# A decayed linear attention with two feed-forward layers: the work around each attention cell in another order of blocks

## The chip, the cores and the metric

The kernel runs on 1 core of one Trainium2 chip. The metric is device time in microseconds of that core; lower is better. Before the change it is 1261.89 us, the median of 3 runs (1261.34 to 1262.25).

## The reference

Three stages follow each other, all in float32, over 4 batches of 768 tokens (3072 tokens, 384 channels, which are 8 heads of 48).

```python
# attention: a state per batch and head, decayed by w, with a bonus u for the present token
cur = np.einsum('bhd,bhe->bhde', u[None] * kt, vt)
y[:, :, t] = np.einsum('bhd,bhde->bhe', rt, state + cur)
state = w[None, :, :, None] * state + np.einsum('bhd,bhe->bhde', kt, vt)
# first layer: 4 experts of 1024 hidden units, all used, weighted by normalised probabilities
h = np.maximum(x @ w1[e], 0.0)
out += p[:, e:e + 1] * (h @ w2[e])
# second layer: 2048 hidden units
h = x @ w_in
g = h * np.cos(h)
out = g @ w_out
```

## The kernel before, in words

The two layers are one stream of *items*. An item is a block of 128 hidden units for up to 512 tokens: three up matmul groups (`m_up`), a relu or a cosine, and, two or three items later, the down matmuls (`m_down`) into three accumulators. The loop over `n` issues the items in order. A product of float32 precision is made of three rounded ones: each operand is split into a high part, rounded by ScalarE, and a low part, the rest, taken by VectorE (`split`, L117 and L118, for x; L504 and L505 for weights, L608 and L609 for the hidden block, `gh` and `gl`). VectorE does the weights' low part in even items, GpSimd in odd ones, up to item 28. The first 8 items take weights and x as they are (`raw_w`, `x_raw`) and need no split. Items with `n` below about 30 have 256 tokens, later ones 512.

The attention is cut into 24 *cells* of 128 tokens of one batch; `i` counts a batch's cells, `b` the batches. The first two cells are worked before the loop (functions `b_...`). Their results are transposed on TensorE by `b_x` (L274), copied by ScalarE (L275), and are the x of the first items. Later cells are worked inside the loop: at item `ONE_AT[c]` TensorE gets the scores and the state of cell `c` and the outputs of cell `c - 1` (`a_one`, `a_visit`; L191, L177, L357, L368), between the item's own matmuls. A visit borrows the tile `hp` that the item does not use, so it waits for the `gl` of the item before. The other steps of a cell are put down in the table `steps`, by item, relative to `p`, the item of the cell before: `a_load_tok` and `a_load_t` load it, `a_kt` (GpSimd, L149) and `a_r` (VectorE, L145) apply the decay, `a_ru` (GpSimd, L153) the bonus, `a_rk` (VectorE, L157) takes the product of both, `a_kp` (VectorE, L166) the keys for the state, `a_sum` (VectorE, L161) the sum of the bonus. `wide` is true for cells 3 to 8, whose visits are 4 items apart; later visits are 3 apart. Within an item, `mix` places these steps between the matmuls; each engine works its own queue in the order in which it was written.

A visit's result goes to DRAM (`yd`). When the four batches of an `i` are done, `x_in` loads it back and queues the three splits of x, with a delay in items (a lag and a step for each of the three parts).

The splits in the loop's head are written before an item's matmuls, the splits of weights after 8 items at its end:

```python
if n < BLK - 3:
    raw_load(n + 3, nc.scalar)
if 2 <= n < BLK:
    w_loads(n - 1)
    w_splits(n - 3, nc.gpsimd if n % 2 else None)
```

Loads of the first blocks are issued from ScalarE's queue (up to three weight blocks and cells 3 to 5), the others from SP's. The tile pools `ps_d` and `ps_u` use the same banks one after the other; `ups2` are the two tiles `hp`.

Of the kernel before, what the change touches and what calls it, by code (L numbers as in the profile page):

```python
# [11 lines left out]
ACTF = mybir.ActivationFunctionType  # L12
ALU = mybir.AluOpType
# [13 lines left out]
def attention_moe_cos_mlp_kernel(  # L27
# [17 lines left out]
    nc = tc.nc  # L45
# [7 lines left out]
    C = 64  # L53
# [5 lines left out]
    BLK = 8  # L59
# [40 lines left out]
    pw = at_p.tile([128, HP, 129], F32, name="pw")  # L100
    w128 = at_p.tile([128, HP, 1], F32, name="w128")
# [12 lines left out]
    dense_ps = [ps_d.tile([128, 2, 512], F32, tag=t, name=f"{t}_ps") for t in ("ds", "dy")]  # L114
# [36 lines left out]
    def a_ru(c):  # L151
        t = ld[c]["tok"][:, 0:2]
        nc.gpsimd.tensor_tensor(out=t, in0=t, in1=uu_ch, op=ALU.mult)  # L153
# [81 lines left out]
    def b_mask(c):  # L235
        s_ = t_p.tile([128, 2, HP, C], F32, tag="s", name="s")
        by = ld[c]["ps"].rearrange("q c (p a t) -> q a c p t", p=HP, a=2)
        wide = [128, 2, HP, C]
        nc.vector.tensor_tensor(out=s_, in0=by[:, 0], in1=mask.unsqueeze(1).unsqueeze(1).to_broadcast(wide), op=ALU.mult)
        nc.vector.copy_predicated(  # L240
            out=s_, mask=eye.bitcast(I32).unsqueeze(1).unsqueeze(1).to_broadcast(wide), data=by[:, 1],
        )
        ld[c]["s"] = s_
# [28 lines left out]
    def b_x(c, px):  # L272
        for kk in range(KD):
            nc.tensor.transpose(px[:, kk * 128:kk * 128 + 128], ld[c]["yo"][:, kk * 128:kk * 128 + 128], ident)  # L274
        nc.scalar.activation(  # L275
            out=x_raw[:, :, c * 128:c * 128 + 128], in_=px[:, 0:DM].rearrange("q (k t) -> q k t", k=KD), func=ACTF.Copy
        )
# [17 lines left out]
    ups2 = []  # L295
# [117 lines left out]
    def x_in(i, j, lag, cols=slice(0, TB), step=None):  # L413
        src = acc[j].rearrange("q b d -> q (b d)").rearrange("q (k t) -> q k t", k=KD)
        nc.sync.dma_start(out=src[:, :, cols], in_=yd[i].rearrange("(k q) t -> q k t", k=KD)[:, :, cols])
        x_split(src, j, lag, cols, step or X_STEP)

    def x_split(src, j, lag, cols=slice(0, TB), step=None):
        for kk in range(KD):
            later.append((  # L420
                lag + (step or X_STEP)[kk],
                lambda kk=kk: split(xh[j][:, kk, cols], xl[j][:, kk, cols], src[:, kk, cols]),
            ))

    def a_x(c):
        b, i = cells[c]
        if b == B - 1 and i == 0:
            x_in(0, 0, X0_LAG, slice(256, 512), (0, 0, 0))
        if b == B - 1 and i == 1:
            x_in(1, 1, XT_LAG)  # L430
        ld.pop(c)

    NC_ = len(cells)
# [8 lines left out]
    on_pe = (a_one,)  # L442
    ONE_AT = {c: 4 * c - 6 for c in range(N_FIRST, 9)}
    ONE_AT.update({c: 29 + 3 * (c - 9) for c in range(9, NC_ + 1)})
    BEGIN = {3: ((a_load_tok, 0), (a_load_t, 0), (a_ru, 1)), 4: ((a_load_tok, 3), (a_load_t, 4), (a_ru, 5)), 5: ((a_load_tok, 6), (a_load_t, 7), (a_ru, 8))}

    def steps_of(c):
        at, p = ONE_AT[c], ONE_AT[c - 1]
        wide = at - p > 3
        two = ONE_AT.get(c - 2, 0)  # L450
        yield from BEGIN.get(c, ((a_load_tok, two - 1), (a_load_t, two), (a_ru, p - (2 if wide else 1))))
        yield from ((a_kt, p), (a_r, p + wide), (a_rk, p + 2), (a_kp, p + 2), (a_sum, p + 2 + wide))

    steps = {}
    for c in range(N_FIRST, NC_ + 1):
# [40 lines left out]
    def raw_load(q, eng=None):  # L496
        (eng or nc.sync).dma_start(out=raw_w[0, 0, q], in_=moe_wb[q])
# [22 lines left out]
    def w_loads(n):  # L520
        while w_nl[0] < min(n, len(w_keys)):
            w_load(w_keys[w_nl[0]])
            w_nl[0] += 1
# [196 lines left out]
    wu_a = const.tile([128, 128], mybir.dt.bfloat16, name="wu_a")  # L720
    wu_b = const.tile([128, 512], mybir.dt.bfloat16, name="wu_b")
# [133 lines left out]
    N_DEC = N_ATT + 4  # L855
    X_STEP = (0, 0, 1)
    X_LAG = 1
    XT_LAG = 2
    TAIL = 2
    Y_LAG = 1  # L860
    WARM_FIRST = 17
    X0_LAG = 2
# [21 lines left out]
    with tc.manual_schedule():  # L884
# [12 lines left out]
        raw_load(1)  # L897
        prob_load()
        raw_load(2)
        for c in range(N_FIRST):  # L900
            b_r(c)
            a_kt(c, nc.vector)
        nc.vector.tensor_tensor(out=w128, in0=pw[:, :, 2 * C:2 * C + 1], in1=pw[:, :, 2 * C:2 * C + 1], op=ALU.mult)
        for c in range(N_FIRST):
            b_ru(c)
        off = x_bank()
# [4 lines left out]
        b_score(1, dense_ps[0], off[:, HP * C:2 * HP * C])  # L911
        b_off(1)
        b_mask(1)
        a_ru(2)
        a_kt(2)
        b_in(0, dense_ps[1][:, :, 0:HD])
# [4 lines left out]
        b_in(1, pair_ps[:, :, 0:HD])  # L921
        b_y(1)
        b_x(0, dense_ps[0][:, 0])
        b_x(1, dense_ps[0][:, 1])
        a_r(2)
        a_rk(2)
        a_sum(2)
# [2 lines left out]
        ps_d_ctx.close()  # L930
        ps_u = ctx.enter_context(tc.tile_pool(name="ps_u", bufs=1, space=bass.MemoryType.PSUM))
        ups2 += [ps_u.tile([128, TB], F32, name=f"hp{x}") for x in range(2)]
        for hp in ups2:
            nc.tensor.matmul(hp[:, 256:512], wu_a, wu_b[:, 0:256], start=True, stop=True)
        ps_a = ctx.enter_context(tc.tile_pool(name="ps_a", bufs=1, space=bass.MemoryType.PSUM))
        downs = []
        pend = []
# [1 line left out]
        for n in range(NI + 4):  # L939
            live = n < NI  # L940
            moe2 = False
            if n < BLK - 3:
                raw_load(n + 3, nc.scalar)
            if 2 <= n < BLK:
                w_loads(n - 1)
                w_splits(n - 3, nc.gpsimd if n % 2 else None)
            if n == 3:
                prob_norm()
# [19 lines left out]
            if live:  # L968
# [21 lines left out]
                hp, ups = m_up(n)  # L990
# [247 lines left out]
```

## Time and profile before

| what | value |
|---|---|
| median of 3 runs | 1261.89 us |
| the profiled execution | 1262.03 us |
| its span, first to last instruction | 1260.3 us |
| TensorE (PE) busy | 1246.5 us, 99% of the span |
| VectorE (DVE) busy | 773.0 us, 61% |
| ScalarE (ACT) busy | 492.9 us, 39% |
| GpSimd (POOL) busy | 193.6 us, 15% |
| granted TensorE clock | 0.999 |

The profile is one execution. A line of its timeline gives the start, the length, the engine, the source line and the operation, what it writes and reads, and, in brackets, how long the engine was idle before it and what ended that. SPq and ACTq are the instructions by which these engines issue transfers. The whole attention lies in the first quarter of the span, up to about 310 us, and VectorE is busy for 219 of the first 300 us.

### The profile page before, as it was taken

How to read it: one execution, taken by the hardware profiler on the slowest of the kernel's cores; microseconds unless marked ns; L12 is line 12 of the kernel's file. 1: busy time of each engine (PE TensorE's matmuls, PEld its weight loads, DVE VectorE, ACT ScalarE, POOL GpSimd, SP SyncE). 2: the span in 40 equal slices, each digit the busy share in tenths (PEclk: the TensorE clock that was granted, in tenths of full speed). 3: DMA queues.
4: the chain of work that ended last, by engine and by line, in shares of the span. 5: the costliest groups of instructions: out<-in, count | busy, mean ns of one | idle time of the engine just before them, and what ended most of it. 6: DMA issues, size and time to landing. Idle time of an engine off the chain costs nothing.

```text
span 1260.3 us, 20498 instructions
## 1 busy us (share of the span) xinstructions
PE 1246.5 (99%) x8453; PEld 1038.8 (82%) x8453; DVE 773.0 (61%) x1259; ACT 492.9 (39%) x879; POOL 193.6 (15%) x190
## 2 busy tenths in 40 slices
PE   9999999999999999999999999999999999999997
PEld 7898888788888888888888888888888888888886
DVE  6897747766264464546645543326776777777665
ACT  4442313223221131112111222216777677767774
POOL 3664323421100000111111111112000100010100
PEclk9999999999999999999999999999999999999999
DMA  8635634444242243223331410123001400160601
GB/s 322 220 117 177 196 125 154 124 137 111 84 139 59 84 134 109 67 76 127 107 92 52 133 43 9 59 78 122 1 1 42 160 26 25 36 203 13 196 11 47
DMA packets 72501, 126.53 MB, mean 100 GB/s; under 512 B 23153, under 2 KB 44754, under 8 KB 72402
## 3 DMA queue, kind: packets, MB, share of 16 engines
q1 hardware_dynamic: 65634, 93.38, 23.6%
q0 software_dynamic: 4608, 25.17, 6.4%
q10 hardware_dynamic: 2160, 6.62, 1.5%
q8 instruction: 67, 1.10, 0.4%
q14 instruction: 32, 0.26, 0.1%
HBM read 101.90 MB, written 23.25 MB: 99 GB/s over the span
## 4 chain that ended last, share of the span: by engine, by line


## 5 line engine op out<-in xcount | busy, mean ns | idle before, releaser
L595 PE MATMUL hp<-xh,w 128*128 128x512 f32 (+1 forms) x888 | 341.3, 384 | 1.6 <-DVE gl L609 1.6
L596 PE MATMUL hp<-xl,w 128*128 128x512 f32 (+1 forms) x888 | 338.1, 381 | 0.5 <-DVE xl L118 0.5
L597 PE MATMUL hp<-xh,w 128*128 128x512 f32 (+1 forms) x888 | 337.9, 380 | 0.2 <-issue 0.2
L670 PE MATMUL a<-gh,w 128*128 128x512 f32 (+1 forms) x880 | 335.0, 381 | 0.0
L671 PE MATMUL a<-gh,w 128*128 128x512 f32 (+1 forms) x880 | 334.8, 380 | 0.0
L672 PE MATMUL a<-gl,w 128*128 128x512 f32 (+1 forms) x880 | 334.7, 380 | 0.0
L608 ACT ACTIVATE gh<-hp 128x512 fp32r<-128x512 f32 (+1 forms) x200 | 114.5, 573 | 539.7 <-PE hp L597 532.6
L609 DVE SCALAR_TENSOR_TENSOR gl<-hp,gh 128x512 fp32r<-128x512 f32 (+1 forms) x200 | 131.1, 657 | 299.5 <-ACT gh L608 298.8
L595 PEld LDWEIGHTS hp<-xh,w 128*128 128x128 f32 x888 | 166.9, 188 | 35.7 <-DVE gl L609 2.9
L597 PEld LDWEIGHTS hp<-xh,w 128*128 128x128 f32 x888 | 166.9, 188 | 32.1
L596 PEld LDWEIGHTS hp<-xl,w 128*128 128x128 f32 x888 | 167.0, 188 | 31.9 <-DVE xl L118 0.7
L670 PEld LDWEIGHTS a<-gh,w 128*128 128x128 f32 x880 | 165.5, 188 | 32.0 <-ACT rr L626 0.4
L672 PEld LDWEIGHTS a<-gl,w 128*128 128x128 f32 x880 | 165.5, 188 | 31.7
L671 PEld LDWEIGHTS a<-gh,w 128*128 128x128 f32 x880 | 165.5, 188 | 31.5
L693 POOL TENSOR_TENSOR acc<-acc,pm 128x512 f32<-128x512 f32 (+1 forms) x57 | 72.5, 1302 | 537.9 <-DVE pm L692 537.9
L628 DVE SCALAR_TENSOR_TENSOR hs<-rr,hs 128x512 f32<-128x512 f32 x96 | 67.4, 702 | 62.8 <-ACT rr L627 62.8
L626 ACT ACTIVATE rr<-rr 128x512 f32<-128x512 f32 x96 | 60.8, 633 | 86.4 <-DVE rr L621 86.4
L620 DVE SCALAR_TENSOR_TENSOR rr<-ni,hs 128x512 f32<-128x512 int32 x96 | 66.3, 691 | 45.6 <-ACT ni L619 45.6
L621 DVE SCALAR_TENSOR_TENSOR rr<-ni,rr 128x512 f32<-128x512 int32 x96 | 66.5, 692 | 3.3
L507 POOL DMA_DIRECT2D w<-dec_all x32 | 17.1, 535 | 333.0 <-PE a L672 332.1
L118 DVE TENSOR_TENSOR gl<-hs,gh 128x512 fp32r<-128x512 f32 x96 | 66.0, 688 | 0.7 <-ACT gh L117 0.7
L618 ACT ACTIVATE hs<-hp 128x512 f32<-128x512 f32 x96 | 57.2, 596 | 17.8 <-PE hp L597 17.6
(151 smaller groups left out, 1066.2 us busy)
## 6 DMA issues: line engine op xcount, KB each, us to landing
w<-dec_all POOLq DMA_DIRECT2D x32, 768.0 KB, 4.6
s<-in_moe_wb_dram SPq DMA_DIRECT2D x53, 384.0 KB, 4.0
draw<-in_moe_wb_dram SPq DMA_DIRECT2D x32, 384.0 KB, 4.3
dec_all<-dout SPq DMA_DIRECT2D x32, 384.0 KB, 3.0
tok<-in_tok_ch_dram SPq DMA_DIRECT2D x19, 576.0 KB, 5.4
rkt<-in_rkt_dram SPq DMA_DIRECT2D x21, 512.0 KB, 3.8
pb<-pn SPq DMA_DIRECT2D x24, 256.0 KB, 5.0
out_dram<-acc SPq DMA_DIRECT2D x17, 256.0 KB, 2.5
```

The lines of the kernel that those rows point to most:

```text
L595: nc.tensor.matmul(hp, wh[:, kk, :], x_h[:, kk, :], start=kk == 0, stop=False)
L596: nc.tensor.matmul(hp, wh[:, kk, :], x_l[:, kk, :], start=False, stop=False)
L597: nc.tensor.matmul(hp, wl[:, kk, :], x_h[:, kk, :], start=False, stop=kk == KD - 1)
L608: nc.scalar.activation(out=gh, in_=hp, func=ACTF.Relu)
L609: nc.vector.scalar_tensor_tensor(out=gl, in0=hp, scalar=0.0, in1=gh.bitcast(F32), op0=ALU.max, op1=ALU.subtract)
L620: nc.vector.scalar_tensor_tensor(out=rr, in0=ni, scalar=-PI2_HI, in1=hs, op0=ALU.mult, op1=ALU.add)
L621: nc.vector.scalar_tensor_tensor(out=rr, in0=ni, scalar=-PI2_LO, in1=rr, op0=ALU.mult, op1=ALU.add)
L628: nc.vector.scalar_tensor_tensor(out=hs, in0=rr, scalar=1.0, in1=hs, op0=ALU.subtract, op1=ALU.mult)
L670: nc.tensor.matmul(a, wh[:, ds], gh, start=q == 0, stop=False)
L671: nc.tensor.matmul(a, wl[:, ds], gh, start=False, stop=False)
L672: nc.tensor.matmul(a, wh[:, ds], gl, start=False, stop=q == BLK - 1)
L693: nc.gpsimd.tensor_tensor(out=o, in0=o, in1=m, op=ALU.add)
```

## The change

Eight edits; line numbers are those of the kernel before.

1. `b_x(1, ...)`: the transposes of the second cell go to the other tile, `dense_ps[1]`.
2. The two matmuls that fill columns 256 to 512 of the tiles `hp` (L934) are gone; two ScalarE copies in items 0 and 1 do it.
3. `w128` is computed after the masks of the first two cells.
4. Weight block 3 is loaded by SP ahead of the loop; blocks 4 to 7 by ScalarE's queue at items 2 to 5, one item later than before, and the weight loads that are split begin one item later.
5. Cell 3: loads at item 1 and bonus at item 2, each one item later.
6. `a_rk` for cells from 9 on one item earlier; unchanged for cells 3 to 8.
7. `a_kp` for cells 3 to 8 one item later; unchanged after that.
8. x parts: the third part of the second half of the first x one item later; the parts of the second x at lags 1, 2, 3, where they were at 2, 2, 3.

```diff
--- before.py
+++ after.py
@@ -425,9 +425,9 @@
     def a_x(c):
         b, i = cells[c]
         if b == B - 1 and i == 0:
-            x_in(0, 0, X0_LAG, slice(256, 512), (0, 0, 0))
+            x_in(0, 0, X0_LAG, slice(256, 512), (0, 0, 1))
         if b == B - 1 and i == 1:
-            x_in(1, 1, XT_LAG)
+            x_in(1, 1, XT_LAG, step=(0, 1, 2))
         ld.pop(c)
 
     NC_ = len(cells)
@@ -442,14 +442,14 @@
     on_pe = (a_one,)
     ONE_AT = {c: 4 * c - 6 for c in range(N_FIRST, 9)}
     ONE_AT.update({c: 29 + 3 * (c - 9) for c in range(9, NC_ + 1)})
-    BEGIN = {3: ((a_load_tok, 0), (a_load_t, 0), (a_ru, 1)), 4: ((a_load_tok, 3), (a_load_t, 4), (a_ru, 5)), 5: ((a_load_tok, 6), (a_load_t, 7), (a_ru, 8))}
+    BEGIN = {3: ((a_load_tok, 1), (a_load_t, 1), (a_ru, 2)), 4: ((a_load_tok, 3), (a_load_t, 4), (a_ru, 5)), 5: ((a_load_tok, 6), (a_load_t, 7), (a_ru, 8))}
 
     def steps_of(c):
         at, p = ONE_AT[c], ONE_AT[c - 1]
         wide = at - p > 3
         two = ONE_AT.get(c - 2, 0)
         yield from BEGIN.get(c, ((a_load_tok, two - 1), (a_load_t, two), (a_ru, p - (2 if wide else 1))))
-        yield from ((a_kt, p), (a_r, p + wide), (a_rk, p + 2), (a_kp, p + 2), (a_sum, p + 2 + wide))
+        yield from ((a_kt, p), (a_r, p + wide), (a_rk, p + 1 + wide), (a_kp, p + 2 + wide), (a_sum, p + 2 + wide))
 
     steps = {}
     for c in range(N_FIRST, NC_ + 1):
@@ -855,7 +855,7 @@
     N_DEC = N_ATT + 4
     X_STEP = (0, 0, 1)
     X_LAG = 1
-    XT_LAG = 2
+    XT_LAG = 1
     TAIL = 2
     Y_LAG = 1
     WARM_FIRST = 17
@@ -897,10 +897,10 @@
         raw_load(1)
         prob_load()
         raw_load(2)
+        raw_load(3)
         for c in range(N_FIRST):
             b_r(c)
             a_kt(c, nc.vector)
-        nc.vector.tensor_tensor(out=w128, in0=pw[:, :, 2 * C:2 * C + 1], in1=pw[:, :, 2 * C:2 * C + 1], op=ALU.mult)
         for c in range(N_FIRST):
             b_ru(c)
         off = x_bank()
@@ -911,6 +911,7 @@
         b_score(1, dense_ps[0], off[:, HP * C:2 * HP * C])
         b_off(1)
         b_mask(1)
+        nc.vector.tensor_tensor(out=w128, in0=pw[:, :, 2 * C:2 * C + 1], in1=pw[:, :, 2 * C:2 * C + 1], op=ALU.mult)
         a_ru(2)
         a_kt(2)
         b_in(0, dense_ps[1][:, :, 0:HD])
@@ -921,7 +922,7 @@
         b_in(1, pair_ps[:, :, 0:HD])
         b_y(1)
         b_x(0, dense_ps[0][:, 0])
-        b_x(1, dense_ps[0][:, 1])
+        b_x(1, dense_ps[1][:, 0])
         a_r(2)
         a_rk(2)
         a_sum(2)
@@ -930,8 +931,6 @@
         ps_d_ctx.close()
         ps_u = ctx.enter_context(tc.tile_pool(name="ps_u", bufs=1, space=bass.MemoryType.PSUM))
         ups2 += [ps_u.tile([128, TB], F32, name=f"hp{x}") for x in range(2)]
-        for hp in ups2:
-            nc.tensor.matmul(hp[:, 256:512], wu_a, wu_b[:, 0:256], start=True, stop=True)
         ps_a = ctx.enter_context(tc.tile_pool(name="ps_a", bufs=1, space=bass.MemoryType.PSUM))
         downs = []
         pend = []
@@ -939,10 +938,12 @@
         for n in range(NI + 4):
             live = n < NI
             moe2 = False
-            if n < BLK - 3:
-                raw_load(n + 3, nc.scalar)
-            if 2 <= n < BLK:
-                w_loads(n - 1)
+            if n < 2:
+                nc.scalar.activation(out=ups2[1 - n][:, 256:512], in_=wu_b[:, 0:256], func=ACTF.Copy)
+            if 2 <= n < BLK - 2:
+                raw_load(n + 2, nc.scalar)
+            if 3 <= n < BLK:
+                w_loads(n - 2)
                 w_splits(n - 3, nc.gpsimd if n % 2 else None)
             if n == 3:
                 prob_norm()
```

The order in which the instructions now stand shows it at three places.

VectorE's queue around items 4 to 6, where cell 3 is prepared (`kp` are the keys, `xl` the low parts of x, L505 a weight's low part). Before:

```order
L505 TENSOR_TENSOR w<-s,w 128x768
L118 TENSOR_TENSOR xl_99<-acc_106,xh_98 128x256
L157 TENSOR_TENSOR tok<-tok 128x384
L166 TENSOR_TENSOR kp_125<-tok,wk_ch 128x384
L118 TENSOR_TENSOR xl_99<-acc_106,xh_98 128x256
L161 TENSOR_REDUCE dsum<-tok 128x8
```

Now:

```order
L505 TENSOR_TENSOR w<-s,w 128x768
L118 TENSOR_TENSOR xl_99<-acc_106,xh_98 128x256
L157 TENSOR_TENSOR tok<-tok 128x384
L118 TENSOR_TENSOR xl_99<-acc_106,xh_98 128x256
L166 TENSOR_TENSOR kp_125<-tok,wk_ch 128x384
L161 TENSOR_REDUCE dsum<-tok 128x8
```

The keys of cell 3 have moved behind the second part of x.

ScalarE's queue at items 3 and 4 (L604 is the relu of a first item, L497 loads a block that stays as it is, L493 a block that L504 will split, L137 and L128 load a cell). Before:

```order
L497 DMA raw_xl_103<-in_moe_wb_dram 128x768
L493 DMA s<-in_moe_wb_dram 128x768
L137 DMA tok<-in_tok_ch_dram 128x1152
L604 ACTIVATE gh<-hp_355 128x256
L497 DMA raw_xl_103<-in_moe_wb_dram 128x768
L493 DMA s<-in_moe_wb_dram 128x768
L504 ACTIVATE w<-s 128x768
```

Now:

```order
L497 DMA raw_xh_102<-in_moe_wb_dram 128x768
L493 DMA s<-in_moe_wb_dram 128x768
L137 DMA tok<-in_tok_ch_dram 128x1152
L604 ACTIVATE gh<-hp_356 128x256
L497 DMA raw_xl_103<-in_moe_wb_dram 128x768
L493 DMA s<-in_moe_wb_dram 128x768
L504 ACTIVATE w<-s 128x768
```

The rows read alike, but each stands for the block before: in the upper list the first L493 loads weight block 1 and the second block 2, in the lower one block 0 and block 1. L504 here rounds block 0 in both.

VectorE's queue at items 23 to 25, where cell 8 is prepared. Before:

```order
L609 SCALAR_TENSOR_TENSOR gl<-hp_355,gh 128x256
L157 TENSOR_TENSOR tok<-tok 128x384
L166 TENSOR_TENSOR kp_127<-tok,wk_ch 128x384
L609 SCALAR_TENSOR_TENSOR gl<-hp_354,gh 128x256
L505 TENSOR_TENSOR w<-raw_xh_102,w 128x768
L161 TENSOR_REDUCE dsum<-tok 128x8
```

Now:

```order
L609 SCALAR_TENSOR_TENSOR gl<-hp_356,gh 128x256
L157 TENSOR_TENSOR tok<-tok 128x384
L609 SCALAR_TENSOR_TENSOR gl<-hp_355,gh 128x256
L505 TENSOR_TENSOR w<-raw_xh_102,w 128x768
L166 TENSOR_TENSOR kp_127<-tok,wk_ch 128x384
L161 TENSOR_REDUCE dsum<-tok 128x8
```

The keys of cell 8 have moved behind the low part of the hidden block and behind that of a weight; the same holds for cells 4 to 7, with or without the weight.

## Rows read from the trace of the kernel before

**Rows 1.** Page, part 1: busy time and share of the engines.
```profile
PE 1246.5 (99%) x8453; PEld 1038.8 (82%) x8453; DVE 773.0 (61%) x1259; ACT 492.9 (39%) x879; POOL 193.6 (15%) x190
```

**Rows 2.** Waits, TensorE: us in total, times, longest.
```profile
PE hp L595 <- DVE gl L609: 1.6, 3, 1.1
...
PE hp L357 <- DVE gl L609: 1.1, 2, 0.7
```

**Rows 3.** Timeline 13 to 16 us, ScalarE and TensorE: start, us, engine, operation, idle before.
```profile
13.28 0.49 ACT L275 ACTIVATE acc<-ds_ps 128x384 f32<-128x384 f32 x1
...
13.83 0.55 PE L274 MATMUL ds_ps<-ident,yo 128*128 128x128 f32 x3 [0.63 <-ACT acc L275]
...
14.95 0.38 PE L934 MATMUL hp<-wu_b,wu_a 128*128 128x256 bf16 x2 [0.58 <-ACT acc L275]
...
15.17 2.75 PE L589 MATMUL hp<-acc,raw_xh 128*128 128x256 f32 x12
```

**Rows 4.** Timeline 22 to 32 us, ScalarE with its queue, VectorE, GpSimd, TensorE.
```profile
22.16 0.45 ACTq L493 DMA_DIRECT2D s<-in_moe_wb_dram  x1
...
23.85 0.38 ACT L604 ACTIVATE gh<-hp 128x256 f32<-128x256 f32 x1 [1.24 <-PE hp L589]
...
27.62 0.55 DVE L166 TENSOR_TENSOR kp<-tok,wk_ch 128x384 f32<-128x384 f32 x1
...
27.77 0.84 ACT L504 ACTIVATE w<-s 128x768 fp32r<-128x768 f32 x1 [0.89 <-DMA s<-in_moe_wb_dram]
...
28.70 1.81 POOL L505 TENSOR_TENSOR w<-s,w 128x768 fp32r<-128x768 f32 x1 [2.62 <-ACT w L504]
...
28.96 1.83 DVE L118 TENSOR_TENSOR xl<-acc,xh 128x256 fp32r<-128x256 f32 x1 [0.80 <-ACT xh L117]
...
30.46 1.19 POOL L153 TENSOR_TENSOR tok<-tok,uu_ch 128x384 f32<-128x384 f32 x1
...
31.16 0.54 PE L177 MATMUL pair_ps<-tok,kp 64*48 64x48 f32 x32
```

**Rows 5.** DMA view at 22.1 us: issue, KB, us to landing.
```profile
s<-in_moe_wb_dram ACTq DMA_DIRECT2D x1, 384.0 KB, 5.6
```

**Rows 6.** Timeline 51 to 54.2 us, GpSimd, VectorE, TensorE.
```profile
51.18 2.16 POOL L505 TENSOR_TENSOR w<-s,w 128x768 fp32r<-128x768 f32 x1
...
51.56 2.19 DVE L166 TENSOR_TENSOR kp<-tok,wk_ch 128x384 f32<-128x384 f32 x1
...
52.59 0.28 PE L671 MATMUL a<-gh,w 128*128 128x256 f32 x1
...
52.71 0.28 PE L672 MATMUL a<-gl,w 128*128 128x256 f32 x1
...
54.14 0.39 PE L595 MATMUL hp<-xh,w 128*128 128x256 f32 x1 [1.15 <-DVE gl L609]
```

**Rows 7.** Timeline 60.5 to 62.2 us, GpSimd, VectorE, TensorE.
```profile
60.58 1.19 POOL L153 TENSOR_TENSOR tok<-tok,uu_ch 128x384 f32<-128x384 f32 x1
...
60.82 1.23 DVE L118 TENSOR_TENSOR xl<-acc,xh 128x256 fp32r<-128x256 f32 x1
...
62.10 0.39 PE L596 MATMUL hp<-xl,w 128*128 128x256 f32 x1 [0.48 <-DVE xl L118]
```

**Rows 8.** Timeline 85 to 88.7 us, GpSimd, VectorE, TensorE.
```profile
85.41 1.33 POOL L153 TENSOR_TENSOR tok<-tok,uu_ch 128x384 f32<-128x384 f32 x1
...
87.40 2.65 POOL L505 TENSOR_TENSOR w<-raw_xl,w 128x768 fp32r<-128x768 f32 x1 [0.66 <-ACT w L504]
...
87.41 0.94 DVE L505 TENSOR_TENSOR w<-raw_xh,w 128x768 fp32r<-128x768 f32 x1
...
88.60 0.40 PE L177 MATMUL pair_ps<-tok,kp 64*48 64x48 f32 x19
```

**Rows 9.** Timeline 233 to 236.5 us, VectorE and TensorE.
```profile
233.40 1.64 DVE L157 TENSOR_TENSOR tok<-tok 128x384 f32<-128x384 f32 x1
...
236.36 0.44 PE L177 MATMUL pair_ps<-tok,kp 64*48 64x48 f32 x20 [0.87 <-DVE kp L166]
```

## The prediction

> **What bounds the kernel now.** I read the page first, then the waits, then the timelines where TensorE waits. The page shows TensorE busy for 1246.5 of a span of 1260.3 us [rows 1]; nothing else is near that, so the end moves only by what TensorE loses or gains. The list of its waits shows how little there is to gain: waits on VectorE's `gl` (the low part of a hidden block, L609) of 1.6 us in front of the up matmuls and of 1.1 us in front of the attention matmuls [rows 2], the others below, with these some 6 us in all, or 0.5% of the span. A wait costs a little more than its row says: matmuls of 256 columns start 0.12 us apart while each is drawn 0.28 us long, so about 0.16 us of the loss is drawn as busy [rows 6]. All times are for this profiled execution (1262.03 us, 0.14 above the median of the runs, 1261.89). A difference under 0.2% (2.5 us) counts as none.
>
> Every edit is meant for one of these waits. So the sum has two kinds of terms: a wait that goes, and a wait that the new order makes.
>
> **Term 1, the second cell's x in its own tile, and the filling matmuls gone: -0.7 us.** The second set of transposes starts at 13.83, released by ScalarE's copy (L275) of 13.28 to 13.77, because both cells write one tile [rows 3]. In a tile of its own it needs only ScalarE's copy before that one, which ended when L275 began, at 13.28: 13.83 - 13.33 = 0.5 us. The two filling matmuls (L934) start at 14.95, the first real one at 15.17: 0.22 us more [rows 3]. Their replacement is two ScalarE copies of 256 columns. They lie behind L275, and ScalarE then waits for TensorE's first block (1.3 us), so they cost nothing there; without that cover each costs one evacuation, 0.38 us (L604 has this size [rows 4]).
>
> **Term 2, the keys of cell 3 behind an x part: +2.6 us, the largest and least certain.** Before, the keys' product `kp` ran at 27.62 for 0.55 us, 3 us before TensorE needed it (L177 at 31.16) [rows 4]. VectorE then waited for `xh` of the second x part and did `xl` at 28.96. In the new order `xl` comes first and `kp` behind it. What `xl` waits for is a chain: the load of a weight block lands, ScalarE rounds it (L504, 27.77, after 0.89 us idle for that load) and then writes `xh`, and VectorE takes 1.83 us for `xl` because GpSimd's L505 runs from 28.70 to 30.51; `xl` ends 0.28 us after that, at 30.79 [rows 4]. The load itself moves too. It was issued at 22.16, ahead of the relu of 23.85; it now stands behind that relu [rows 4], which comes 0.7 us earlier by term 1, so it is issued at 23.1 to 23.5. With its 5.6 us to landing [rows 5] that is 28.7, 0.9 us later than 27.77, at least as late as before at the lower bound (the transfers ahead of it keep the queue full), so `xl` ends between 30.8 and 31.7. GpSimd's next operation (L153) stands ready at that moment, as at 30.46 [rows 4], and takes 0.9 to 1.0 us; if it comes first, `kp` ends 0.4 us behind it. Lower bound: 30.8 + 0.4 = 31.2; upper: 31.7 + 0.9 + 0.4 = 33.0. TensorE wants it at 31.16 - 0.73 = 30.4. The wait is 0.8 to 2.6 us. I take the upper end, since the only row with a VectorE operation standing behind another while a GpSimd operation is ready (60.58 before 60.82 [rows 7]) shows GpSimd going first. Below the lower bound only an earlier landing helps, and nothing issues this load earlier.
>
> The rest of the spread loads I cost at nothing: `raw` block 3 goes to SP's queue, which had nothing to do there, and later blocks are used after the visit that term 2 delays. A new point is the first weight block on SP: its issue now also waits for the store of `pn`, and the block behind it for the `yd` stores. ScalarE reaches that rounding some 4 us later than the issue, so what covers it is the delay of term 2; without that delay it costs up to 0.4 us, one rounding (0.84 us [rows 4]) less the slack.
>
> **Term 3, cell 5 and the x parts of 14 to 16: -0.3 us.** Here `kp` took 2.19 us, to 53.75, because GpSimd's L505 held on to 53.34; `gl` stood behind it, and TensorE started at 54.14 instead of 52.71 + 0.12 + 0.1 [rows 6]. With `gl` ahead of `kp` this wait goes: -1.2 us, and `kp` still ends at 53.75, just before its use. The next `gl`, behind the sum, makes the visit wait 0.2 us. But the third x part now stands behind the decay product L145 (0.7 us). It ended at 62.05, and TensorE went on at 62.10 [rows 7]. All that follows the visit moves 1.0 us forward, this part 0.7 back: 61.8. So of 1.0 us only 0.3 is left.
>
> **Term 4, cell 8: -0.3 us, by a hair.** With `gl` first, another `gl` wait goes (-0.5, what the 1.6 us leave beside the longest of 1.1 [rows 2]); the sum and its `gl` then come 0.2 us late. `kp` now stands behind VectorE's L505, which can follow GpSimd's L153 of 85.41 to 86.74, takes 0.87 us and ends at 87.6; GpSimd's L505 is ready at 87.40 [rows 8]. If `kp` goes first, it ends at 88.0, in time for TensorE's L177 (88.60, now 88.15 [rows 8]). The nearest row decides: at 87.40 and 87.41 both asked, and VectorE's 0.94 us ran undisturbed while GpSimd's 1.8 us (28.70 [rows 4]) became 2.65 [rows 8]. So GpSimd's start in the record is a little earlier than its claim.
>
> **Term 5, cells 9 and later: -1.2 us.** The bonus product L157 moves one block forward. In the block at 233 us it stood at 233.40, behind a weight part, took 1.64 us, and `kp` behind it made TensorE wait 0.87 us at 236.36 [rows 9]; then came a `gl` wait of about 0.4. Done a block earlier, it leaves its place to `kp`, which ends at 235.0, in time: -1.0, and -0.2 of the second. Cells 9 and 10 have 256-column blocks, so L157 ahead of `gl` can cost what it takes, 0.5 us, and spreading the second x can give back at most the longest attention wait, 0.7 [rows 2]; I take 0. The other cells have 512 columns and no wait to lose.
>
> Sum: -0.7 + 2.6 - 0.3 - 0.3 - 1.2 = +0.1; 1262.1 us in this execution, 1262.0 against the runs.
>
> **Rivals.**
> *GpSimd wins at cell 8.* Then `kp` waits for all of L505: 87.6 + 1.75 + 0.4 = 89.75, where TensorE wants it at 88.15, and the next `gl` is 0.4 us late again: +1.4 instead of -0.3, 1263.7 us; with the 0.5 of cell 9 and the 0.4 of SP, 1264.6. It decides from a lead of GpSimd of 0.1 to 0.2 us. For it: the 0.24 us lead at 60.58 was enough [rows 7]; against it: 0.01 was not [rows 8]. [...]
>
> *The waits go and no new one binds.* If the load lands early and `kp` of cell 3 gets in with its lower bound, term 2 is +0.8 and the sum -1.7: 1260.2 us. If `kp` of cell 3 does not wait at all, and the spreading also frees the second x (-0.7): 1258.7 us. For it: each edit stands at a wait of the list. Against it: the chain load, L504, `xh`, `xl`, `kp` has no slack in the rows.
>
> *The order does less than it says.* If term 2's delay only shifts VectorE's and GpSimd's work with it, terms 3 to 5 give nothing and terms 1 and 2 remain: 1263.8 us. Against it: by 45 us VectorE waits for TensorE's visit, so the two are in step again.
>
> **How the numbers follow.** Forecast, 1261 to 1263.2: 0.40. GpSimd wins at cell 8: 0.25, half of it over 1264.4. No new wait binds: 0.25, most of it under 1259.4 when the second x is freed too. Less than it says: 0.10, a fifth over 1264.4 with the bounds of cell 9 and SP. The range 1258.4 to 1264.9 leaves out the ends of the second and third case, about 0.1 each. Faster: 0.22 (nearly all of the third case). Slower: 0.19 (half of the second, with some of the fourth and of unseen waits). The same: 0.59.
>
> **What would show it.** Term 1: no L934, up matmuls at 14.5. Term 2: a wait of TensorE's L177 on `kp` near 30.5 to 33 us; if it is missing, the forecast is wrong downwards. Term 3: no `gl` wait near 53, a longer `xl` wait near 61. Term 4: `kp` of cell 8 near 88 (0.5 us) or near 90 (2 us). Term 5: no `kp` wait near 236. A wait on a weight part's load or on ScalarE's roundings between 35 and 45 us would mean that SP's queue was costed wrongly.

## The result: slower by 7 us, and the profile after

| | before | after |
|---|---|---|
| median of 6 runs | 1262.54 us (1261.34 to 1263.30) | 1269.62 us (1268.49 to 1271.16) |
| ratio after / before | | 1.0058, 95% interval 1.0045 to 1.0071 |
| profiled execution, its span | 1262.03, 1260.3 us | 1269.11, 1267.3 us |

The forecast was 1262.0, in a range of 1258.4 to 1264.9; the measured time lies above it. Of the 79 runs of the kernel before that stand beside the experiments below, 16 took 1264.0 to 1268.5 us, so a ratio there can differ from that of the medians; no trace of such a run is kept. The page of the changed kernel, parts 1 and 2 (busy time; granted TensorE clock, in tenths, in 40 slices of the span):

```profile
PE 1250.1 (99%) x8451; PEld 1040.8 (82%) x8451; DVE 775.8 (61%) x1259; ACT 493.3 (39%) x881; POOL 191.8 (15%) x190
...
PEclk9899999999999999999999999999999999999999
```

The engines have the work they had [rows 1]; the second slice, near 32 to 63 us, shows a lower clock (8 tenths). TensorE's waits in the changed kernel (us in total, times, longest):

```profile
PE pair_ps L177 <- DVE kp L166: 5.0, 2, 3.6
PE hp L595 <- DVE gl L609: 1.6, 3, 0.8
...
PE hp L596 <- DVE xl L118: 1.0, 1, 1.0
PE hp L589 <- ACT acc L275: 0.6, 1, 0.6
PE pair_ps L177 <- issue: 0.3, 1, 0.3
PE hp L357 <- DVE gl L609: 0.2, 1, 0.2
```

Of the waits of before [rows 2], that of the attention matmuls on `gl` fell from 1.1 to 0.2, and that of the up matmuls is the same in sum, at other places. In their place stand 5.0 us on the keys. To see where the time went, take the start of the same matmul in both traces and follow the difference, after less before:

| place in the trace of before | difference, us | what made the step |
|---|---|---|
| 7.1, first attention matmul | +0.9 | the 17 warm-up matmuls took 6.66 us, not 5.80, and the trace's record of the clock, 1.00, begins at 7.1, not 5.4; ahead of every edit |
| 15.2, first up matmul | +0.1 | term 1, -0.7 |
| 19.8, first visit | +1.1 | two waits at "issue", +0.9 |
| 31.2, visit of cell 3 | +4.8 | wait for the keys, +3.8 |
| 33.9 | +7.3 | half clock, +2.5 |
| 54.1, cell 5 | +6.0 | wait on `gl` gone, -1.3 |
| 62.1, x part | +6.9 | visit's `gl` +0.4, x part +0.5 |
| 88.6, cell 8 | +8.0 | `gl` -0.5, wait for the keys +1.5 |
| 96.8 and 105.4, cells 9 and 10 | +9.6 | two waits on `gl`, +0.8 and +0.9 |
| 108.3 | +8.6 | visit's `gl` gone, -1.0 |
| 237.4, end | +7.3, +7.5 | keys' wait and part of the next gone, -1.3 |

Cell 3, which the prediction called its largest and least certain step, in the timeline of the changed kernel (start, us, engine, operation, idle before):

```profile
24.94 0.39 ACT L604 ACTIVATE gh<-hp 128x256 f32<-128x256 f32 x1 [1.72 <-PE hp L589]
...
25.32 0.74 ACTq L493 DMA_DIRECT2D s<-in_moe_wb_dram  x1
...
31.68 0.84 ACT L504 ACTIVATE w<-s 128x768 fp32r<-128x768 f32 x1 [2.18 <-DMA s<-in_moe_wb_dram]
...
32.60 1.80 POOL L505 TENSOR_TENSOR w<-s,w 128x768 fp32r<-128x768 f32 x1 [5.40 <-ACT w L504]
...
32.86 1.82 DVE L118 TENSOR_TENSOR xl<-acc,xh 128x256 fp32r<-128x256 f32 x1 [2.15 <-ACT xh L117]
...
34.36 1.17 POOL L153 TENSOR_TENSOR tok<-tok,uu_ch 128x384 f32<-128x384 f32 x1
...
34.60 1.34 DVE L166 TENSOR_TENSOR kp<-tok,wk_ch 128x384 f32<-128x384 f32 x1
...
36.00 0.90 PE L177 MATMUL pair_ps<-tok,kp 64*48 64x48 f32 x32 [3.57 <-DVE kp L166]
```

This is the forecast chain link by link, GpSimd's L153 ahead of `kp` included, but the load was issued at 25.3, not at 23.1 to 23.5, and landed 6.3 us later where 5.6 were taken [rows 5]. TensorE stood still for 3.6 us, and then came what the prediction had no term for. The same kernel in four stretches (length, busy time of PE, PEld, DVE, ACT, POOL with counts, then the granted clock, DMA share, GB/s):

```profile
20.00:32.00 12.00, 11.74 (x125) 10.06 (x119) 6.26 (x12) 3.44 (x9) 5.06 (x6) 1.00 0.97 342
32.00:34.40 2.40, 0.43 (x32) 0.29 (x21) 1.54 (x1) 1.10 (x3) 1.80 (x2) 1.00 0.90 327
34.40:41.20 6.80, 5.20 (x86) 4.57 (x87) 6.07 (x10) 2.99 (x8) 2.25 (x4) 0.50 0.21 51
41.20:53.00 11.80, 11.80 (x172) 10.80 (x171) 4.88 (x10) 4.00 (x7) 5.91 (x5) 1.00 0.94 330
```

From 34.4 to 41.2 the granted clock is 0.50, called half clock here, after TensorE had been busy for 0.43 of 2.40 us. Cell 8, the race that the prediction gave to VectorE:

```profile
94.30 1.82 POOL L505 TENSOR_TENSOR w<-raw_xl,w 128x768 fp32r<-128x768 f32 x1 [0.66 <-ACT w L504]
...
94.37 2.16 DVE L166 TENSOR_TENSOR kp<-tok,wk_ch 128x384 f32<-128x384 f32 x1
...
96.58 0.57 PE L177 MATMUL pair_ps<-tok,kp 64*48 64x48 f32 x32 [1.46 <-DVE kp L166]
```

GpSimd led by 0.07 us and VectorE's 0.55 us became 2.16. And the cell that had waited at 236.36 [rows 9]:

```profile
235.97 0.55 DVE L157 TENSOR_TENSOR tok<-tok 128x384 f32<-128x384 f32 x1
...
241.99 1.64 DVE L166 TENSOR_TENSOR kp<-tok,wk_ch 128x384 f32<-128x384 f32 x1
...
243.92 0.54 PE L177 MATMUL pair_ps<-tok,kp 64*48 64x48 f32 x32
```

Here the bonus product is done a block earlier, and TensorE finds the keys ready, as forecast.

### The profile page after: what moved, and what is told of

Same layout as the page of the kernel before. It is cut to its first block, busy times and chain, and to the rows that moved or that the text cites. A ratio compares the mean times of both kernels' runs of the same rounds, so it can differ in the third digit from the quotient of the medians.

```text
span 1267.3 us, 20509 instructions
## 1 busy us (share of the span) xinstructions
PE 1250.1 (99%) x8451; PEld 1040.8 (82%) x8451; DVE 775.8 (61%) x1259; ACT 493.3 (39%) x881; POOL 191.8 (15%) x190
## 3 DMA queue, kind: packets, MB, share of 16 engines
q1 hardware_dynamic: 65778, 93.77, 23.6%
## 4 chain that ended last, share of the span: by engine, by line
## 5 line engine op out<-in xcount | busy, mean ns | idle before, releaser
L118 DVE TENSOR_TENSOR gl<-hs,gh 128x512 fp32r<-128x512 f32 x96 | 66.0, 687 | 0.7 <-ACT gh L117 0.7
```

## The experiments

All ratios are against the kernel before, run on the same chip; times are medians. The first four kernels and the sixth are the change with one thing altered, the others the kernel before with one thing altered. The listings show the altered lines alone, or the parts of a line that differ.

**The keys of cell 3 back ahead of the x part.**

```diff
-(a_kp, p + 2 + wide)
+(a_kp, p + 2 + (wide and c != 3))
```

> The change, with the keys of cell 3 back ahead of the second x part (its block 5); all else as changed. Theory A (the new place of these keys makes both the wait of 3.6 us at 32.4 us and the half clock behind it): TensorE goes on at about 32.4, the clock stays at 1.0 through 34 to 41 us, and 6.3 us go (3.8 of wait, 2.5 of half clock): 1263.3 us. Theory B (the spread loads are late by themselves): the wait only moves on, to the fourth x part or the first split weight blocks near 36 to 40 us, which the stall covered; then the clock may fall there, and the time stays above 1265.

1270.58 us, ratio 1.0054 (1.0037 to 1.0071): nothing gained. The wait at 32 us is gone, but two others are there, in TensorE's list:

```profile
PE pair_ps L177 <- DVE kp L166: 3.9, 2, 2.4
PE pair_ps L177 <- issue: 3.1, 1, 3.1
```

The longest wait for keys is now at cell 4, 2.4 us at 49 us: ScalarE stood for 4.3 us for a weight block that landed at 49.3, VectorE's low part of it stood behind, and the keys behind that. Theory B had such a wait, on the spread loads, though it looked for it earlier. The wait at "issue", for nothing that the profile shows, lies in the first visit at 19.6 us, in the midst of matmuls that need nothing new; after it the clock is 0.5 from 22.1 to 28.9. Neither theory had that.

**The loads back at their old places, keys as changed.**

```diff
-        raw_load(3)
-            if 2 <= n < BLK - 2:
-                raw_load(n + 2, nc.scalar)
-            if 3 <= n < BLK:
-                w_loads(n - 2)
+            if n < BLK - 3:
+                raw_load(n + 3, nc.scalar)
+            if 2 <= n < BLK:
+                w_loads(n - 1)
```

(and cell 3's loads as before)

> The change, with the loads of the first blocks back at their old places (raw block 3 on ScalarE's queue, the first weight blocks issued one block earlier, the loads of cell 3 in block 0); the keys of cell 3 stay behind the x part. Theory A (the late load and the new place of the keys make the wait only together): the second weight block lands near 28.5 instead of 31.6, the keys end at 31 to 32.4, TensorE waits at most 0.6 us, the clock stays at 1.0, and about 6 us go: 1263.5 us. Theory B (the new place of the keys is enough, as the prediction's step on cell 3 had it, 2.6 us): a wait of 2 to 2.6 us near 32 stays, 1265.5 with the clock at 1.0 or 1268 with a half clock behind it.

1267.35 us, 1.0032 (1.0017 to 1.0047). The wait for the keys of cell 3 is gone, but a wait at "issue" of 3.6 us at 19.3 us precedes it and delays TensorE by as much, so this kernel can't say what the keys' place costs alone. That was tried later.

**TensorE kept at work through the wait of cell 3.**

```diff
     def a_visit(c):
+        if c == 2:
+            for _ in range(32):
+                nc.tensor.matmul(ups2[1 - item[0] % 2][:, 256:512], wu_a, wu_b[:, 0:256], start=True, stop=True)
```

> The change, with 32 matmuls of 256 bf16 columns (zeros, into PSUM columns that nothing reads at that time) ahead of the visit of cell 3, at 0.108 us each 3.5 us: TensorE works through the wait for the keys instead of standing still; the keys end when they did. Theory A (the half clock of 34.4 to 41.3 us follows from TensorE standing still): the visit starts at 36.0 to 36.2 as before, the clock stays at 1.0, and 2.5 us go: 1267.1 us. Theory B (the half clock has another cause, such as the start of the attention visit, or is of this execution): the clock falls all the same, 1269.6 us.

1272.63 us, 1.0072 (1.0052 to 1.0092), with 3.3 us at "issue" at 19.2 us again. The clock stayed at 1.00 through the filled wait, as theory A has it:

```profile
32.00:38.40 6.40, 5.83 (x73) 4.81 (x75) 4.38 (x4) 2.57 (x5) 2.95 (x2) 1.00 0.64 245
```

But it also stayed at 1.00 in the next kernel behind an unfilled wait of 3.4 us at the same place. So the filling isn't shown to be what kept it.

**Keys of cell 8 and bonus products of cells 9 and 10 back.**

```diff
-(a_rk, p + 1 + wide), (a_kp, p + 2 + wide)
+(a_rk, p + 1 + (wide or c in (9, 10))), (a_kp, p + 2 + (wide and c != 8))
```

> The change, with the keys of cell 8 and the bonus products of cells 9 and 10 back at their old places; the wait of cell 3 stays. By the offsets between the two traces: cell 8 costs +0.95 in the change (a wait on the hidden block of 0.46 gone, one on the keys of 1.54 come, 0.13 behind it), cell 9 +0.79, cell 10 +0.93. Theory A (each of these waits is made by its edit): 2.7 us go, 1266.9 us, with the keys' wait at 95 us gone, no wait on the hidden block at 104.5, and one at 114 gone. Theory B (VectorE and GpSimd only stand otherwise by the 7 us of delay, and the waits come from that): they stay, 1269 to 1270 us.

1269.46 us, 1.0044 (1.0030 to 1.0059). By the trace, the keys' wait of cell 8 and the wait on `gl` at cell 9 are gone, and at cell 10 two waits on `gl` of 0.3 are left: theory A at its places, but for a new wait at "issue" of 0.5 us that ends at 96.4. The time does not show it: the ratio is 0.0014 less than that of the change, some 1.8 us, but the intervals overlap and the medians differ by 0.2 us. The profiled execution, without a half clock, is the fastest of the ten (1266.13 us). The clock behind the wait of cell 3, same kernel:

```profile
34.40:41.20 6.80, 5.61 (x99) 5.04 (x100) 6.31 (x9) 4.05 (x9) 3.13 (x4) 1.00 0.29 73
```

**Term 1 alone**, in the kernel before (and `w128` later):

```diff
-        b_x(1, dense_ps[0][:, 1])
+        b_x(1, dense_ps[1][:, 0])
-        for hp in ups2:
-            nc.tensor.matmul(hp[:, 256:512], wu_a, wu_b[:, 0:256], start=True, stop=True)
+            if n < 2:
+                nc.scalar.activation(out=ups2[1 - n][:, 256:512], in_=wu_b[:, 0:256], func=ACTF.Copy)
```

> The kernel before, with only the first part of the change: the second cell's x in its own tile, the two filling matmuls replaced by ScalarE copies, w128 later. Theory C (TensorE's instruction packets come late once this part has gone, a wait with no semaphore at the 705th instruction of TensorE's records, 0.5 to 3.8 us long in all five traces of changed kernels and absent in the kernel before): the wait is there, near 19 to 23 us, with or without a half clock behind it, and the kernel is slower than before by 0 to 4 us: about 1264. Theory D (as predicted, this part alone gains 0.7 us; the late packets come from the other loads): no such wait, 1261.6 us.

1266.35 us, 1.0032 (1.0020 to 1.0043): slower by 4 us. Theory C. In its timeline the visit is cut in two:

```profile
19.30 0.37 PE L177 MATMUL pair_ps<-tok,kp 64*48 64x48 f32 x16
23.28 0.57 PE L177 MATMUL pair_ps<-tok,kp 64*48 64x48 f32 x15 [3.61 <-issue]
```

and behind it, in a window of the same trace, TensorE runs at half clock:

```profile
22.60:29.40 6.80, 6.12 (x28) 4.96 (x28) 3.23 (x7) 0.94 (x3) 2.98 (x3) 0.50 0.43 140
```

What does TensorE wait for? The traces point to its own program. DMA queue 8 carries packets of 16 KB (1.10 MB in 67) that the profile calls "instruction". With 256 instructions in each, as the places below suggest, these are 17152, against 17030 records of TensorE in the kernel before; so the queue is taken to be TensorE's. The page of the kernel before and of the change has them in part 3 (packets, MB, share of 16 engines):

```profile
q8 instruction: 67, 1.10, 0.4%
```

The trace gives their start and end, and TensorE's records (weight loads, matmuls and recorded semaphore waits, counted in order) give the place:

| kernel | 449th record | packet on the queue | 705th record could start | it starts |
|---|---|---|---|---|
| before | 15.06 | 16.66 to 18.21 | 19.75 | 19.75 |
| the change | 15.97 | 18.42 to 19.29 | 20.4 | 20.86 |
| term 1 alone | 14.81 | 20.78 to 21.66 | 19.5 | 23.28 |
| keys of cell 3 back | 14.59 | 20.50 to 21.45 | 19.6 | 22.88 |
| loads back | 14.82 | 20.67 to 21.56 | 19.3 | 23.11 |

In all four changed kernels of the table TensorE waits at the 705th record, 256 behind the 449th, and it goes on 1.4 to 1.6 us after the packet's end. The change also waits at the 449th, some 0.4 us, and there too goes on 1.5 us after a packet's end (14.51). These two waits of the change are those at "issue" in the table of differences. In the kernel before, 18.21 + 1.5 is 19.7: the packet came just as it was needed in this execution.

**The filling matmuls kept, the rest as changed.**

```diff
+        for hp in ups2:
+            nc.tensor.matmul(hp[:, 256:512], wu_a, wu_b[:, 0:256], start=True, stop=True)
-            if n < 2:
-                nc.scalar.activation(out=ups2[1 - n][:, 256:512], in_=wu_b[:, 0:256], func=ACTF.Copy)
```

> The change, with the two filling matmuls kept where they were and the two ScalarE copies left out. Theory C1 (the late packet hangs on these two matmuls alone): no wait without a semaphore at 19 to 23 us; the wait for the keys of cell 3 stays, 3.6 us at 32 us; time about 1268 with a half clock, 1266 without. Theory C2 (what matters is when TensorE and the bulk loads reach that place, and TensorE still comes 0.5 us earlier than before by the separate tile): the wait of 0.5 to 3.8 us stays, 1268 to 1272.

1271.60 us, 1.0072 (1.0050 to 1.0094), from 4 runs. The wait at the 705th record is 0.4 us in this profile: theory C2, a little under its lower end. The filling matmuls alone don't decide whether the wait is there. The seven traced kernels with the separate tile all wait there, 0.4 to 3.8 us; the five traced with one tile and the old borders don't. All seven also have the later `w128`, which was not tried apart, so the tile is the likely cause and not a shown one.

**The same work with 40 more instructions of TensorE.**

```diff
-        for _ in range(n):
+        for _ in range(n - 1):
             nc.tensor.matmul(hp, wu_a, wu_b, start=True, stop=True)
+        for _ in range(21):
+            nc.tensor.matmul(hp[:, 0:24], wu_a, wu_b[:, 0:24], start=True, stop=True)
```

> The kernel before, with one of its 17 warm-up matmuls of 512 columns cut into 21 of 24 columns: the same work, but 40 more instructions of TensorE (20 matmuls, each with its weight load), so that every later instruction stands 40 places further on in TensorE's program. Theory T (TensorE's instructions come in packets of 16 KB with borders at the 193rd, 449th and 705th record, and TensorE waits where it reaches a border less than some 5 us after the one before): the border at 449 now falls to 12.2 us, 3.7 us after the one at 193 (8.5); a wait without a semaphore of 1 to 2 us at the 449th record, none at the 705th (7 us after it), 1263 to 1264.5 us. Theory U (the wait at 20 us belongs to the attention visit that stands there and not to a border): no such wait at 12 us, the records up to 20 us within 0.3 of before, 1262.3 us.

1267.07 us, 1.0032 (1.0018 to 1.0047). Theory T, to the record, though 2.6 us over its time, which had no half clock: TensorE stops at the 449th, now in the attention of the first two cells, where it never waited before, and not at the 705th:

```profile
13.09 0.28 PE L259 MATMUL pair_ps<-tok,acc 64*64 64x48 f32 x4
15.39 0.33 PE L253 MATMUL pair_ps<-tok,s 64*64 64x48 f32 x8 [2.01 <-issue]
```

Its packet ended at 13.95, 1.4 us earlier. A half clock (0.50) from 16.8 to 23.6 follows. By the difference of the traces this kernel is 0.9 us late at its first attention matmul, ahead of the border, then loses 2.3 at the border and 2.7 by the half clock. So moving a packet's border by 40 instructions, with nearly the same work, costs 4 us by the ratio and 4.9 by the medians, the half clock included.

**The spread loads alone**, in the kernel before (and cell 3's loads and bonus one item later):

```diff
+        raw_load(3)
-            if n < BLK - 3:
-                raw_load(n + 3, nc.scalar)
-            if 2 <= n < BLK:
-                w_loads(n - 1)
+            if 2 <= n < BLK - 2:
+                raw_load(n + 2, nc.scalar)
+            if 3 <= n < BLK:
+                w_loads(n - 2)
```

> The kernel before, with only the loads of the first blocks spread out (raw block 3 on SyncE's queue, the first weight blocks one block later, the loads of cell 3 in block 1). The keys of cell 3 stand ahead of the x part, so a late weight block can't hold them. Theory G (the prediction's: the spread loads cost nothing or up to 0.4 us): 1262.3 to 1262.7, TensorE's records up to 60 us within 0.4 us of before. Theory H (the loads land 2 to 3 us later, as the second weight block did in the change, 31.6 for 27.8, and the x parts and the first split weight blocks behind them are late for the block at 43 us): a wait of 1 to 2 us near 36 to 45 us, 1264.

1267.77 us, 1.0042 (1.0030 to 1.0054): theory H, and more than it said. At the visit of cell 4:

```profile
45.02 0.84 ACT L504 ACTIVATE w<-s 128x768 fp32r<-128x768 f32 x1 [4.64 <-DMA s<-in_moe_wb_dram]
...
45.77 0.37 ACT L608 ACTIVATE gh<-hp 128x256 fp32r<-128x256 f32 x1
...
45.90 0.96 DVE L505 TENSOR_TENSOR w<-s,w 128x768 fp32r<-128x768 f32 x1 [3.84 <-ACT w L504]
...
47.24 0.41 DVE L609 SCALAR_TENSOR_TENSOR gl<-hp,gh 128x256 fp32r<-128x256 f32 x1
...
47.70 0.25 PE L357 MATMUL hp<-s,tok 64*48 64x64 f32 x1 [2.65 <-DVE gl L609]
```

This weight block went out on SP's queue at 39.79, where before it went at 36.66 and landed 0.39 us late at 41.77. The relu of the hidden block stands behind its rounding on ScalarE, and `gl` behind its low part and a sum on VectorE, so the visit waits. Half clock (0.50) follows, 48.9 to 52.3, and costs another 1.5 us by the difference of the traces (4.3 at 47.7, 5.8 at 52.2). At the visit of cell 3 the difference already rises by some 0.9, with a wait on a relu (L604) of 0.6.

**The keys of cell 3 alone**, in the kernel before:

```diff
-(a_kp, p + 2)
+(a_kp, p + 2 + (c == 3))
```

> The kernel before, with only the keys of cell 3 one block later, behind the second x part; loads and everything else as before. Theory P (the prediction's chain, without the late load): the weight block lands as before (rounded from 27.8), the x part's low half ends near 30.8, the keys end at 31.2 to 32.2, TensorE waits 0 to 1.1 us at 31.2: 1262.3 to 1263.4 us, no half clock. Theory Q (the keys' new place makes the whole wait of 3.6 us by itself): a wait over 3 us at 31, with or without a half clock behind it, 1265 to 1268 us.

1263.98 us, 1.0008 (0.9992 to 1.0025). By the trace:

```profile
31.80 1.17 POOL L153 TENSOR_TENSOR tok<-tok,uu_ch 128x384 f32<-128x384 f32 x1
...
32.05 1.34 DVE L166 TENSOR_TENSOR kp<-tok,wk_ch 128x384 f32<-128x384 f32 x1
...
33.45 0.57 PE L177 MATMUL pair_ps<-tok,kp 64*48 64x48 f32 x32 [1.30 <-DVE kp L166]
```

Theory P, with a wait 0.2 us over its end (1.3 us) and full clock. The interval of the ratio reaches below 1, so it is the trace and not the time that shows the cost. The 3.6 us of the change need both the keys' new place and the late load.

**The keys of cell 8 and the bonus products of cells 9 and 10 alone**, in the kernel before:

```diff
-(a_rk, p + 2), (a_kp, p + 2)
+(a_rk, p + 2 - (c in (9, 10))), (a_kp, p + 2 + (c == 8))
```

> The kernel before, with only the keys of cell 8 one block later and the bonus products of cells 9 and 10 one block earlier. Theory R (GpSimd's weight part is first when both are ready, as in four of the five traces with this order): the keys of cell 8 take 2.1 us and TensorE waits 1.4 to 1.7 us for them near 88.5, less 0.46 for the hidden block, and waits of 0.8 to 0.9 on the hidden block near 97 and 106 (the second in place of the 0.9 at 107.3): 1263.8 us. Theory S (the prediction's): VectorE is first at cell 8, the keys take 0.55 us, 0.3 us are gained there, and cells 9 and 10 cost 0 to 0.5: 1262.2 us.

1264.47 us, 1.0013 (1.0003 to 1.0023). Theory R at cell 8:

```profile
87.54 1.82 POOL L505 TENSOR_TENSOR w<-raw_xl,w 128x768 fp32r<-128x768 f32 x1 [0.66 <-ACT w L504]
...
87.62 2.16 DVE L166 TENSOR_TENSOR kp<-tok,wk_ch 128x384 f32<-128x384 f32 x1
...
89.83 0.57 PE L177 MATMUL pair_ps<-tok,kp 64*48 64x48 f32 x32 [1.46 <-DVE kp L166]
```

In all six traces with this order GpSimd leads by 0.07 to 0.09 us and wins. A half clock from 91.0 to 94.4 costs 1.4 us more (difference of the traces 1.2 at 89.8, 2.6 at 94.5). Cells 9 and 10 cost 0.2 at 108.2 and give 0.4 back at the visit: theory R had them too dear. That TensorE, late by 2.6 there, gives VectorE the time is the likely reason, not a shown one.

**Three late parts alone**: the keys of cell 5, the bonus products from cell 11 on, the second x's parts.

```diff
-(a_rk, p + 2), (a_kp, p + 2)
+(a_rk, p + (2 if c < 11 else 1)), (a_kp, p + 2 + (c == 5))
-            x_in(1, 1, XT_LAG)
+            x_in(1, 1, XT_LAG, step=(0, 1, 2))
-    XT_LAG = 2
+    XT_LAG = 1
```

> The kernel before, with only three late parts of the change: the keys of cell 5 one block later, the bonus products of the cells from 11 on one block earlier, the second token tile's x parts spread over three blocks. By the offsets between the traces of before and of the change these places gave 1.33 - 0.37 (cell 5), 0.99 (second x) and 1.26 (the cell at 236 us). Theory E (these parts work without the others): nothing changes before 50 us, no wait without a semaphore at 20 us, no half clock, and 2.6 to 3.2 us go: 1259.4 us. Theory F (the gains only stood in the 7 us of delay of the change): no wait of the list goes, 1262.3.

1259.99 us, 0.9982 (0.9970 to 0.9994): faster than both kernels, than the one before by 0.2%. Theory E, a little under its range: no half clock, and behind the 1.3 us of the start TensorE's longest waits are

```profile
PE hp L597 <- issue: 0.6, 1, 0.6
PE ds_ps L274 <- ACT acc L275: 0.6, 1, 0.6
PE hp L595 <- DVE gl L609: 0.6, 2, 0.3
PE hp L934 <- ACT acc L275: 0.6, 1, 0.6
```

The difference of the traces falls by 1.3 at cell 5, rises by 0.35 at its visit and by 0.5 at 90 us (an instruction packet, 0.8 us late), and ends at -1.8.

## Why the prediction was wrong, step by step

In the profiled execution of the change the largest misses are the half clock (+2.5, for which the sum had no term), cell 8 (+1.3 for -0.3), the keys of cell 3 (+3.8 for +2.6) and the two waits for instruction packets (+0.9, no term). Another 0.9 us is the longer warm-up (6.66 us, not 5.80); the record of the clock begins in the 13 traces anywhere from 4.2 to 7.2 us. In order of the terms:

**Term 1, -0.7 us: the step that failed first.** The size at its place was right: the difference falls by 0.73 between 7 and 15 us. What was missing is that TensorE's instructions come in packets (16 KB on the queue, a border at the 449th and the 705th record), and that the one for the first visit arrived with no slack: in the trace of before it ended at 18.21, and the 705th record starts at 19.75, 1.5 us later, as in the kernels where TensorE waited for it (1.4 to 1.6). Alone, this part is slower by 4.1 us; in the profiled execution of the change the packets cost 0.9. In the seven traces with the separate tile the wait at the 705th record is 0.4 to 3.8 us.

**Term 2, +2.6 us: the sign right, the loads wrong.** The chain `xl`, L153, `kp` came as written, GpSimd first. Alone, the keys' new place measured a wait of 1.3 us, inside 0.8 to 2.6. The upper end of the prediction was worked out from the earliest issue alone: 23.5 + 5.6 is 29.1, which makes it 3.0. In the change the load came later still, since the relu ahead of it came at 24.94 and not at 23.15: term 1's 0.7 us, on which this rested, had been lost again to the longer warm-up and the packets, 0.9 us each. The step "the rest of the spread loads I cost at nothing", with "up to 0.4 us" for SP's queue, was mis-sized: alone it costs 5.5 us by the median, and in its trace 2.9 us are the wait of the visit of cell 4. The prediction bounded that wait by one rounding less a slack, and did not follow the load to the relu behind it on ScalarE and to `gl` on VectorE. Together with the keys the late load made 3.6 us at cell 3, which then hid the wait at cell 4. The cover that the prediction named was real; it was as dear as what it covered.

**Term 3, -0.3 us: right.** The wait on `gl` of cell 5 went (-1.3 for -1.2), the visit's rose by 0.4 (0.2 forecast), the x part by 0.5 (0.7).

**Term 4, -0.3 us: wrong side of the race.** The rival "GpSimd wins" was right, with +1.3 by the trace (-0.5, +1.5 and +0.2) for its +1.4. The prediction let a lead of 0.01 us in one row [rows 8] decide. By its own estimate GpSimd stood ready at 87.40 and VectorE at 87.6, and in the six traces with this order GpSimd leads by 0.07 to 0.09 us and goes first. The pair at 60.58 was not the only row of its kind, as the prediction had it. The trace of before also has this one, where GpSimd leads by 0.05 us and takes 1.19 us (1.18 in its shortest rows), and VectorE's L505 takes 1.96 us, for 0.94 in rows 8:

```profile
93.54 1.19 POOL L149 TENSOR_TENSOR rkt<-rkt,pw 128x512 f32<-128x512 f32 x1
93.59 1.96 DVE L505 TENSOR_TENSOR w<-raw_xl,w 128x768 fp32r<-128x768 f32 x1
```

In the 13 traces, up to 250 us, take GpSimd's L149, L153 and L505 against VectorE's L118, L157, L166 and L505: where GpSimd leads by 0.04 to 0.10 us in the record it goes first (48 pairs), and where it leads by 0.03 or less VectorE does (8 pairs, the one in rows 8 among them). So a lead of 0.01 in the record told nothing about one of 0.1.

**Term 5, -1.2 us: right at 236 us** (-1.3 in the trace). Cells 9 and 10, taken as 0 between +0.5 and -0.7, came to +1.7 - 1.0 = +0.7 in the change.

**No term: the clock.** The prediction priced a wait at its length. In the twelve traces with an edit TensorE's idle time shows 16 waits of 1.4 to 3.6 us (the filled one left out), and during or soon after 12 of them a stretch at a granted clock of 0.50 begins, which cost 1.4 to 3.0 us more where it was worked out. In the trace of before the longest wait is 1.3 us, and none comes with such a stretch. Which of them bring it isn't settled: at cell 3 a wait of 3.6 us did (the change) and one of 3.4 us did not (cells 8 to 10 back). That standing still is the cause is argued from this, not shown; the filled wait does not decide it. In the kernel with term 1 alone the clock fell at 22.55, with TensorE still waiting.

The parts do not add up: by the medians they give, alone, +4.1, +5.5, +1.8, +2.3 and -2.2 (against 1262.22), in all +11.5, where the change measures +7.1. Two reasons are in the rows: a TensorE that is late by one wait finds the next thing ready, as cell 4 in the change, and half clocks seem to come in some executions and not in others (the granted clock of the runs of one kernel, cells 8 to 10 back, lies between 0.996 and 0.999). The later keys of cells 4, 6 and 7 and the later third part of the first x were not run alone.

Open: why the packet's transfer begins 0.5 to 1.9 us after the 449th record in the kernels with one tile, and 2.4 to 6.0 us after it in those with two. Bulk loads on the same DMA engines are one candidate; in the change those were nearly idle from 16 to 18 us (DMA share 0.04, 15 GB/s) and the packet began at 18.4 all the same. It wasn't tried further.

## What to carry to other kernels

A wait that is removed near the start of a program can be worth nothing, or less, if the next thing has no slack (term 1 alone: 0.7 us gained at its place, 4.1 lost in all), and the next thing can be the program itself: count TensorE's instructions, and see how fast it runs through them where many small matmuls stand together (here 256 records, from the 449th to the 705th, in 4.7 us before the change). Follow a delayed load through the queue of every engine to the last reader behind it, not only to its own (with the spread loads alone, from a weight block to `gl` and a wait of 2.65 us). Price a long wait of TensorE with the slower clock that may follow (0.50 during or soon after 12 of 16 waits here, 1.4 to 3.0 us more), and take edits one at a time: of the five groups here one was good, and it was good alone.

## What the runs showed that was not expected

Forty more small instructions in the warm-up, with nearly the same work, cost 4.9 us (1267.07 against 1262.22): in the trace 2.3 us of waiting for a packet at the 449th record and the half clock after it. In the kernel before, three such packets come between 12.2 and 23.7 us, each 0.9 to 1.6 us long, and TensorE starts the 449th and the 705th record 1.8 and 1.5 us after the end of the packet that holds them: at the start of this program it runs with next to no slack against the arrival of its own instructions.
